# Raw weight tiles in a free activation buffer, and a new written order of the first slots, in a fused attention and MLP kernel

## The chip, the cores and the metric

The kernel runs on one core of a Trainium2 chip. The metric is the device time of one execution in microseconds (us), lower being better. The engines are named as the profile names them: PE is TensorE (matmuls), DVE is VectorE, ACT is ScalarE, POOL is GpSimd, and SP is SyncE, which here only issues DMAs.

## The reference, cut to what matters

```python
# q, k, v: (4, 8, 576, 64) float32; all four MLP weights float64
kv  = np.einsum('bhsd,bhse->bhde', k, v)
out = np.einsum('bhsd,bhde->bhse', q, kv)
rms = np.sqrt(np.mean(out * out, axis=-1, keepdims=True) + 1e-06)
x   = (out / rms * g_norm).astype(np.float32)      # reordered to (2304, 512)

h = x @ w_in                                       # (2304, 2048)
sp = np.where(h > 20.0, h, np.log1p(np.exp(np.minimum(h, 20.0))))
x = (h * np.tanh(sp) @ w_out).astype(np.float32)   # mish, back to (2304, 512)

h = x @ w2_in
g = np.maximum(h, 0.0) + alpha * np.minimum(h, 0.0)
y = (g @ w2_out).astype(np.float32)
```

## The kernel before, in words

**Stages.** An attention without softmax makes the 2304 x 512 activations x, a first MLP (512 to 2048 to 512, with mish) follows, then a second one (with alpha). This case lies in the first 200 us, where attention of the first tokens, the preparation of the first MLP's weights and the first MLP itself run beside each other.

**Tokens and slots.** The first MLP works through blocks of 512, 256, 512, 512 and 512 tokens (BLOCKS, L34), and within a block through 16 slots, one for each 128 of the 2048 hidden features. Slot s holds mm1(s), 12 matmuls into a tile h, and mm2(s - 4), 12 matmuls into four accumulators acc0 to acc3 (L467 to L489). Each product of fp32 numbers is three matmuls, since both operands are split into a high and a low half (`three`, L128 to L132). Between the two, ScalarE makes n = mish(h) (L505) and its high half gh (L498), and VectorE the low half gl (L499).

**Weights.** A weight tile arrives as raw float64, 512 KB: w1(j) by L381, w2(j) by L378. ScalarE scales the high words (`w_scale`, L390), VectorE makes one fp32 word of two in three instructions (`w_bits`, L396, L397, L400, tile wf), ScalarE casts the high half (`w_high`, L435) and VectorE subtracts the low half (`w_low`, L439). A raw tile lies in a ring of three places (`stage`, L363 to L364), and a load has to wait until the last of the three `w_bits` instructions has read what was there. SP issues the loads in their written order, so one that waits holds back those behind it. The raw tiles of the first slots lie elsewhere (`room`, L143).

**x.** The split activations of a block fill one of the two places of the tile x (L353); until block 1 is made the second place is empty.

**What sets the order.** The order of every engine is written out. For the first four slots two tables do it: FIRST (loads; p: k, v and q of a head pair, c: raw chunk of the first four w1 tiles, w4 and w5: w1(4) and w1(5), u0 and u1: w2(0) and w2(1)) and START, with one word for each step: K a kv product, k its copy out of PSUM (L224), l and n the steps of the norm's root (L294 and L297 on ScalarE, L301 on VectorE), x and y the two halves of a quarter of x (L358, L363), Pcj the three matmuls of quarter c of h(j), g mish, G the split of its result, and A, D, H, L scale, bits, high and low half of a weight (Du1 is `w_bits` of w2(1)). Slots 4 to 19 run through `slot` (L961), which plays lists of steps that L884 to L949 fill by slot number; behind that only PE's order is written.

**Banks.** The tile h(3) lies in the PSUM bank of acc3 (L470), so the last three of the 12 matmuls of mm2(0) wait until mish(3) has read h(3).

Of the kernel before, what the change touches and what calls it, by code (L numbers as in the profile page):

```python
# [11 lines left out]
I32 = mybir.dt.int32  # L12
# [13 lines left out]
P = 128  # L26
# [7 lines left out]
EARLY = 4  # L34
WHEN = {1: (8, 3, 1, 2, 3, 6), 2: (4, 4, 1, 2, 3, 6), 3: (0, 5, 1, 2, 4, 5), 4: (0, 5, 1, 2, 4, 5)}
MANUAL = 20
# [3 lines left out]
UNITS = (36, 45, 52, 61, 65, 68, 70, 85)  # L40
ON_POOL = (0, 1, 2, 3, 5)
BY32 = 2
FIRST = "p0 c0 p1 c1 p2 p3 c2 c3 w4 u0 w5 u1".split()
START = """
W9 K0 k0 W1 T0 t0 W2 Ac0 O0 Dc0 s0 W2 K1 M0 k1 Hc0 Lc0 T1 l0 t1 n0 O1 V f0 K2 s1 x0 M1 k2 Ac1 y0 T2 l1
Dc1 t2 n1 O2 f1 K3 s2 Hc1 M2 k3 x1 Lc1 Ac2 T3 y1 l2 P01 Dc2 P02 t3 P12 n2 Hc2 O3 Ac3 f2 s3 M3 Lc2 x2
y2 P00 P03 Dc3 P10 P11 P13 l3 P20 P21 Z n3 Hc3 f3 P22 P23 Lc3 x3 Aw4 y3 Au0 Dw4 P30 P31 P32 P33 g0
G0 Hw4 Lw4 Du0 g1 G1 Hu0 Aw5 Lu0 g2 Dw5 Au1 Hw5 Du1 Lw5
""".split()


# [1 line left out]
def attn_moe_moe2(  # L53
# [30 lines left out]
    nc = tc.nc  # L84
    B, H, S, D = q.shape
    NT, DM = out.shape
# [6 lines left out]
    TM = max(BLOCKS)  # L93
# [11 lines left out]
    xp = ctx.enter_context(tc.tile_pool(name="xp", bufs=2))  # L105
# [17 lines left out]
    acol = const.tile([P, NJ], F32, name="acol")  # L123
# [93 lines left out]
    def kv_of(b, p):  # L217
        return kvs[(NP * b + p) % len(kvs)]

    def kv_ev(b, p):  # L220
        ps = at.pop(("kv", b, p))
        for hs in (slice(0, D), slice(D, P)):
            if b == 0:
                nc.vector.tensor_copy(out=kv_of(b, p)[hs, hs], in_=ps[hs, hs])  # L224
            else:
                nc.scalar.copy(out=kv_of(b, p)[hs, hs], in_=ps[hs, hs])
# [138 lines left out]
    def stage(nm, dt, cols):  # L365
        return st.tile([P, 2 * DM], dt, tag="ws", name=nm, bufs=3)[:, :cols]


    w1, w2 = {}, {}
    wst, wraw = {}, {}  # L370
    home = {}

    def load_w(L, which, j, early=False, s=None):


        s = s if s is not None else room("ws", I32, 2 * DM) if early else stage("ws", I32, 2 * DM)
# [64 lines left out]
    begun = []  # L441
# [162 lines left out]
    def load_unit(i, n):  # L604
        load_w(1, 1, 2 * i + n, s=place(i, f"r{n}"))
# [45 lines left out]
    def load_out(j):  # L651
        load_w(1, 2, j, s=wp.tile([P, 2 * DM], I32, tag=f"w2{j}", name="ws"))
# [232 lines left out]
    for i in range(1, NB):  # L885
# [24 lines left out]
        for p in range(NP):  # L910
            add(hook, h + db + p, b_pe, i, p)
            add(hook, h + db + p, b_ev, i, p)
    early_w = [({"w": 1, "u": 2}[n[0]], int(n[1:])) for n in FIRST if n[0] in "wu"]
    for j in range(NJ):
        if j >= EARLY and (1, j) not in early_w:
            add(late, max(j - 3, EARLY), load_w, 0, 1, j)
            add(mid, j - 2, w_begin, 0, 1, j)
        if (2, j) not in early_w:
            add(early, max(j + 1, EARLY), load_w, 0, 2, j)
            add(last, j + 2, w_begin, 0, 2, j)  # L920
            add(mid, j + 3, w_end)
        add(early, max(NS - NJ + max(j, EARLY) + 1, UNITS[j // 2] + (6 if j // 2 < NU - 1 else 14)), fetch, 1, j)
        t0 = NS - 8 + 3 * j // 2 if j < SOON else NS + OUTS[j - SOON]
        add(early, t0 - (2 if j < SOON else 4), load_out, j)
        add(fin, t0, behind, prep_out, j, j < SOON)
    for i, s in enumerate(UNITS):
        if i in ON_POOL:
            steps, puts = (1, 2, 2, 3, 4, 5), (4, 5, 6)
        else:
            steps, puts = ((1, 2, 2, 2, 3, 4), (3, 4, 5)) if i < NU - 1 else ((3, 4, 7, 7, 8, 11), (8, 9, 12))  # L930
        add(late, s, load_unit, i, 0)
        add(late, s + 1, load_unit, i, 1)
        for step in range(6):
# [11 lines left out]
    for n in range(1, NPASS):  # L945
        t0 = NS + 4 * NU * n
# [93 lines left out]
    with tc.manual_schedule():  # L1040
        nc.scalar.preload_act_table_set("abs_reciprocal_sqrt_and_small")
        for n in FIRST:
            if n[0] == "p":
                load_kv(0, int(n[1]))
                load_q(0, int(n[1]))
            else:
                load_w(0, code[n[0]], int(n[1:]), True)
            if n == "p1":
                for h in range(2):
                    nc.sync.dma_start(out=gcol[h * D : (h + 1) * D, :], in_=g_norm.rearrange("(p o) -> p o", o=1))  # L1050
        nc.sync.dma_start(out=acol, in_=alpha.rearrange("(j p) -> p j", p=P))
        make_identity(nc, ident)
        nc.vector.memset(ones_bd, 0.0)
        nc.vector.memset(ones_m, 0.0)
        for h in range(2):
            r = slice(h * D, (h + 1) * D)
            nc.vector.memset(ones_bd[r, r], 1.0 / D)
            nc.vector.memset(ones_m[r, 16 * h : 16 * h + 16], 1.0 / D)
        nc.vector.memset(epsb, EPS * 2.0**-SHIFT)
        nc.gpsimd.memset(keep[:, : 5 * P], 0.0)  # L1060
        nc.vector.memset(neglo, 0.0)
        for p in range(NP):
            for h in range(2):
                r = 32 * p + 16 * h
                rows = pick[p][:, h * D : (h + 1) * D]
                nc.vector.tensor_copy(out=rows, in_=ident[:, r : r + 1].to_broadcast([P, D]))
                nc.vector.tensor_tensor(
                    out=rows, in0=f32(rows), in1=ident[:, r + 1 : r + 2].to_broadcast([P, D]), op=ALU.add
                )
                nc.vector.tensor_tensor(out=neglo, in0=neglo, in1=ident[:, r + 1 : r + 2], op=ALU.subtract)  # L1070
        for n in START:
            if n[0] in "ADHL":
                w = (0, code[n[1]], int(n[2:]))
                first[n[0]](*w)
            else:
                first[n[0]](*(int(c) for c in n[1:]))
        begun.append((0, 2, 1))
        for s in range(EARLY, MANUAL):
            slot(s)
    with tc.manual_schedule(engines={mybir.EngineType.PE}):  # L1080
# [34 lines left out]
```

## Time and profile before

| | us |
|---|---|
| median of 3 runs | 856.82 (856.34 to 858.07) |
| profiled execution, its own time | 856.71 |
| its span | 854.8 |
| PE busy | 832.7 (97%) |
| DVE busy | 537.1 (63%) |
| ACT busy | 314.1 (37%) |

The span goes from the first to the last instruction on the chip; the execution's own time is 1.9 us longer. A row of the timeline gives an instruction's start, its duration, engine and line, output and input tile, and in brackets how long its engine stood idle before it and what it waited for last. Busy shares over the whole program are means over stages of different kinds, so the stages are looked at apart.

### The profile page before, as it was taken

Reading aid. Unit: us, or ns where it says so; the run is one execution under the profiler, and the core shown is the slowest. Engines: PE = TensorE matmul, PEld = TensorE weight load, DVE = VectorE, ACT = ScalarE, POOL = GpSimd, SP = SyncE. Lnnn points to the kernel's source line nnn. Section 1 sums busy time; section 2 is a strip of 40 time slices with the busy share of each in tenths; the row PEclk is TensorE's granted clock in tenths of the full one; section 3 lists DMA queues with packets and bytes.
Section 4 is the critical chain, followed back from the end, with each engine's and each line's share of the span. In section 5 each row is a group of like instructions: output and inputs, shape, how many; then the busy total and the mean of one; then the engine's idle time right before and its main releaser. Section 6 shows DMA issues by size and latency. Waiting matters only on the chain.

```text
span 854.8 us, 11671 instructions
## 1 busy us (share of the span) xinstructions
PE 832.7 (97%) x4408; PEld 711.5 (83%) x4408; DVE 537.1 (63%) x1017; ACT 314.1 (37%) x619; POOL 41.8 (5%) x52
## 2 busy tenths in 40 slices
PE   7999889989999999999999999999999999999997
PEld 5677668888878887888888888888988988998896
DVE  6988966372246242635697887889665568655644
ACT  4766445434333443234465323234211124111111
POOL 0000000000210303020300000000000000000000
PEclk9999999999999999999999999999999999999999
DMA  9766454414331233026996623241321231411212
GB/s 250 222 172 205 139 150 102 110 27 106 100 112 25 77 109 135 1 94 231 404 357 231 209 63 134 97 137 39 125 61 38 62 123 39 140 44 38 74 38 74
DMA packets 84744, 104.59 MB, mean 122 GB/s; under 512 B 34768, under 2 KB 58832, under 8 KB 84688
## 3 DMA queue, kind: packets, MB, share of 16 engines
q1 hardware_dynamic: 84688, 103.84, 39.2%
q8 instruction: 35, 0.57, 0.3%
q14 instruction: 21, 0.17, 0.1%
HBM read 79.70 MB, written 24.12 MB: 121 GB/s over the span
## 4 chain that ended last, share of the span: by engine, by line
PE 82%; DVE 8%; DMA 4%; SPq 2%; ACT 2%; issue 1%; DVEq 0%; ACTq 0%
PE acc L130 13%; PE acc L132 13%; PE acc L131 13%; PE h L130 7%; PE h L131 6%; PE h L132 6%; PE pp L130 6%; PE pp L132 6%; PE pp L131 6%; DMA v<-in_v_dram 2%; SPq L183 2%; PE kvps L214 1%; DVE wf L397 1%; DVE wf L400 1%; DMA k<-in_k_dram 1%
## 5 line engine op out<-in xcount | busy, mean ns | idle before, releaser
L130 PE MATMUL acc<-gh,w 128*128 128x512 f32 (+1 forms) x320 | 119.6, 374 | 0.8 <-ACT n L505 0.4
L132 PE MATMUL acc<-gh,w 128*128 128x512 f32 (+1 forms) x320 | 118.0, 369 | 0.0
L131 PE MATMUL acc<-gl,w 128*128 128x512 f32 (+1 forms) x320 | 117.9, 369 | 0.0
L499 DVE TENSOR_TENSOR gl<-n,gh 128x512 fp32r<-128x512 f32 (+1 forms) x80 | 52.2, 652 | 89.9 <-ACT gh L498 89.6
L130 PE MATMUL h<-x,w 128*128 128x512 f32 (+1 forms) x240 | 91.5, 381 | 5.6 <-ACT n L505 5.6
L132 PE MATMUL h<-x,w 128*128 128x512 f32 (+1 forms) x240 | 89.7, 374 | 0.6 <-DVE w L439 0.5
L131 PE MATMUL h<-x,w 128*128 128x512 f32 (+1 forms) x240 | 89.6, 373 | 0.0
L132 PE MATMUL acc<-w,g 128*128 128x512 f32 x216 | 85.4, 395 | 0.0
L498 ACT CAST gh<-n 128x512 fp32r<-128x512 f32 (+1 forms) x80 | 46.1, 577 | 100.4 <-PE acc L132 99.9
L766 ACT CAST g<-ty 128x384 fp32r<-128x384 f32 x48 | 24.7, 515 | 138.4 <-DVE ty L764 136.5
L130 PEld LDWEIGHTS acc<-gh,w 128*128 128x128 f32 x320 | 60.3, 188 | 11.9 <-ACT n L505 0.9
L132 PEld LDWEIGHTS acc<-gh,w 128*128 128x128 f32 x320 | 60.3, 188 | 10.6 <-DVE w L439 0.4
L131 PEld LDWEIGHTS acc<-gl,w 128*128 128x128 f32 x320 | 60.4, 189 | 9.6
L505 ACT ACTIVATE n<-h 128x512 f32<-128x512 f32 (+1 forms) x80 | 44.5, 556 | 45.3 <-DVE gl L499 44.6
L130 PEld LDWEIGHTS h<-x,w 128*128 128x128 f32 x240 | 45.9, 191 | 17.3 <-ACT n L505 6.9
L131 PE MATMUL acc<-w,g 128*128 128x512 f32 x144 | 56.6, 393 | 0.0
L131 PE MATMUL acc<-w,xb 128*128 128x512 f32 x144 | 56.6, 393 | 0.0
L130 PE MATMUL acc<-w,g 128*128 128x512 f32 x144 | 56.0, 389 | 0.0
L130 PE MATMUL acc<-w,xb 128*128 128x512 f32 x144 | 56.0, 389 | 0.0
L132 PEld LDWEIGHTS h<-x,w 128*128 128x128 f32 x240 | 45.9, 191 | 9.5 <-DVE w L439 1.6
L131 PEld LDWEIGHTS h<-x,w 128*128 128x128 f32 x240 | 45.8, 191 | 7.4
L132 PEld LDWEIGHTS acc<-w,g 128*128 128x128 f32 x216 | 40.5, 188 | 9.4 <-DVE g L767 0.9
(216 smaller groups left out, 1700.2 us busy)
## 6 DMA issues: line engine op xcount, KB each, us to landing
xb<-wd SPq DMA_DIRECT2D x72, 256.0 KB, 2.7
ws<-in_moe_w_out_dram SPq DMA_DIRECT2D x32, 512.0 KB, 4.3
ws<-in_moe_w_in_dram SPq DMA_DIRECT2D x16, 512.0 KB, 4.8
r<-in_moe_w_in_dram SPq DMA_DIRECT2D x12, 512.0 KB, 3.9
wd<-r SPq DMA_DIRECT2D x12, 512.0 KB, 2.6
w<-wd SPq DMA_DIRECT2D x12, 512.0 KB, 6.0
k<-in_k_dram SPq DMA_DIRECT2D x16, 288.0 KB, 3.8
v<-in_v_dram SPq DMA_DIRECT2D x16, 288.0 KB, 4.2
```

Source lines behind the costliest of these rows:

```text
L130: nc.tensor.matmul(ps, lh, rh, start=start, stop=False, **kw)
L131: nc.tensor.matmul(ps, lh, rl, start=False, stop=False, **kw)
L132: nc.tensor.matmul(ps, ll, rh, start=False, stop=stop, **kw)
L183: nc.sync.dma_start(out=t[r : r + 32, C * p0 : C * (p0 + n)].rearrange("p (b d) -> p b d", d=32), in_=q[b, h, s : s + C * n, d : d + 32].r ...
L214: nc.tensor.matmul(ps[hs, hs], kt[:, h, j, :], vt[:, h, j, :], start=(j == 0), stop=(j == KVJ - 1))
L397: nc.vector.scalar_tensor_tensor(out=si, in0=high, scalar=-0x80000000, in1=si, op0=ALU.bitwise_and, op1=ALU.bitwise_or)
L400: nc.vector.scalar_tensor_tensor(out=si, in0=high, scalar=3, in1=si, op0=ALU.logical_shift_left, op1=ALU.bitwise_or)
L498: nc.scalar.copy(out=gh, in_=g)
L499: nc.vector.tensor_tensor(out=gl, in0=g, in1=f32(gh), op=ALU.subtract)
L505: nc.scalar.activation(out=g, in_=hps.pop(kk)[:, :T], func=AF.Mish)
L766: nc.scalar.copy(out=h, in_=out)
```

## The change

Seven edits.

1. The START order is written anew, and FIRST brings c2 ahead of p3.
2. ON_ACT: the kv copies of head pairs 1, 2 and 3 (two instructions each) go from VectorE to ScalarE.
3. XW: the raw tiles of w1(6) to w1(13) go to four places in the empty x tile (`xw`) instead of the ring of three. w1(6) and w1(7) are loaded at the end of FIRST, w1(8) to w1(13) up to five slots ahead instead of three.
4. w2(j) is loaded one slot earlier, from slot 4 on.
5. w1(14) and w1(15) still go through the ring, loaded three slots ahead as before.
6. Cast and low half of w2(1) (Hu1, Lu1) stand in START instead of slot 4 (`begun.append` is gone).
7. The small load of alpha goes from the start to slot 19.

```diff
-FIRST = "p0 c0 p1 c1 p2 p3 c2 c3 w4 u0 w5 u1".split()
+FIRST = "p0 c0 p1 c1 p2 c2 p3 c3 w4 u0 w5 u1 w6 w7".split()
+ON_ACT = (1, 2, 3)
+XW = range(6, 14)
...
-G0 Hw4 Lw4 Du0 g1 G1 Hu0 Aw5 Lu0 g2 Dw5 Au1 Hw5 Du1 Lw5
...
+Du0 G0 P33 Hw4 Lw4 g1 Hu0 Lu0 G1 g2 Au1 Dw5 Hw5 Lw5 Du1 Hu1 Lu1
...
@@ kv_ev @@
-            if b == 0:
+            if b == 0 and p not in ON_ACT:
                 nc.vector.tensor_copy(out=kv_of(b, p)[hs, hs], in_=ps[hs, hs])
...
+    xw = xp.tile([P, 8 * TM], I32, tag="x", name="xw")
...
@@ load_w @@
+        if s is None and (L, which) == (0, 1) and j in XW:
+            n = (j - XW[0]) % 4
+            s = xw[:, n * 2 * DM : (n + 1) * 2 * DM]
         s = s if s is not None else room("ws", I32, 2 * DM) if early else stage("ws", I32, 2 * DM)
...
-            add(late, max(j - 3, EARLY), load_w, 0, 1, j)
+            add(late, max(j - (5 if j in XW else 3), EARLY), load_w, 0, 1, j)
+        if j > EARLY + 1:
             add(mid, j - 2, w_begin, 0, 1, j)
         if (2, j) not in early_w:
-            add(early, max(j + 1, EARLY), load_w, 0, 2, j)
+            add(early, max(j, EARLY), load_w, 0, 2, j)
...
+    add(early, MANUAL - 1, lambda: nc.sync.dma_start(out=acol, in_=alpha.rearrange("(j p) -> p j", p=P)))
...
-        nc.sync.dma_start(out=acol, in_=alpha.rearrange("(j p) -> p j", p=P))
...
-        begun.append((0, 2, 1))
```

Behind the edits all line numbers are higher by 2 to 8: L390 becomes L397, L396, L397 and L400 become L403, L404 and L407, L435 becomes L442, L439 becomes L446, L505 becomes L512, L381 and L378 become L388 and L385. PE's order changes in START alone: six matmuls of quarter 0 of h go ahead of the third head pair's attention product, and others of START change places. POOL's order stays.

**ScalarE, end of START and slot 4.** Here w20, w21 and w15 are the split tiles of w2(0), w2(1) and w1(5), and n the results of mish. Before, from the cast of w2(0) on:

```order
L435 CAST w20_461<-wf_451 128x512
L390 ACTIVATE ws_140<-ws_140 128x512
L505 ACTIVATE n_465<-h_359 128x512
L390 ACTIVATE ws_142<-ws_142 128x512
L435 CAST w15_472<-wf_467 128x512
L252 COPY qT_513<-tps_510 128x256
L505 ACTIVATE n_519<-h_384 128x512
L390 ACTIVATE ws_515<-ws_515 128x512
L435 CAST w21_526<-wf_474 128x512
```

and now, where n_467 is mish(2) and n_524 mish(3):

```order
L442 CAST w20_460<-wf_444 128x512
L505 CAST gh_463<-n_458 128x512
L512 ACTIVATE n_467<-h_364 128x512
L397 ACTIVATE ws_143<-ws_143 128x512
L442 CAST w15_474<-wf_470 128x512
L442 CAST w21_481<-wf_477 128x512
L254 COPY qT_520<-tps_517 128x256
L512 ACTIVATE n_524<-h_318 128x512
```

The cast of w2(1) has moved from behind mish(3) (n_519 before) to a place ahead of it and ahead of the copy of qT.

**VectorE, the same place.** Here wf_467 (now wf_470) are the bits of w1(5), wf_474 (now wf_477) those of w2(1), wf_522 (now wf_527) those of w1(6). Before:

```order
L396 TENSOR_SCALAR wf_467<-ws_140 128x512
L397 SCALAR_TENSOR_TENSOR wf_467<-ws_140,wf_467 128x512
L400 SCALAR_TENSOR_TENSOR wf_467<-ws_140,wf_467 128x512
L396 TENSOR_SCALAR wf_474<-ws_142 128x512
L397 SCALAR_TENSOR_TENSOR wf_474<-ws_142,wf_474 128x512
L400 SCALAR_TENSOR_TENSOR wf_474<-ws_142,wf_474 128x512
L439 TENSOR_TENSOR w15_472<-wf_467,w15_472 128x512
L396 TENSOR_SCALAR wf_522<-ws_515 128x512
L397 SCALAR_TENSOR_TENSOR wf_522<-ws_515,wf_522 128x512
L400 SCALAR_TENSOR_TENSOR wf_522<-ws_515,wf_522 128x512
L439 TENSOR_TENSOR w21_526<-wf_474,w21_526 128x512
```

and now:

```order
L403 TENSOR_SCALAR wf_470<-ws_141 128x512
L404 SCALAR_TENSOR_TENSOR wf_470<-ws_141,wf_470 128x512
L407 SCALAR_TENSOR_TENSOR wf_470<-ws_141,wf_470 128x512
L446 TENSOR_TENSOR w15_474<-wf_470,w15_474 128x512
L403 TENSOR_SCALAR wf_477<-ws_143 128x512
L404 SCALAR_TENSOR_TENSOR wf_477<-ws_143,wf_477 128x512
L407 SCALAR_TENSOR_TENSOR wf_477<-ws_143,wf_477 128x512
L446 TENSOR_TENSOR w21_481<-wf_477,w21_481 128x512
L403 TENSOR_SCALAR wf_527<-xw_95 128x512
```

The low half of w1(5) has moved ahead of the bits of w2(1), and the low half of w2(1) ahead of the bits of w1(6).

**SP, the last loads of the first MLP's weights.** L381 and L378 (now L388 and L385) are loads of w1 and w2 tiles; ws_955 is w1(13), ws_1012 w1(14), ws_1069 w1(15), and now ws_1006 is w1(14) and ws_1063 w1(15). Before:

```order
L381 DMA ws_955<-in_moe_w_in_dram 128x4x256
L378 DMA ws_994<-in_moe_w_out_dram 128x1024
L381 DMA ws_1012<-in_moe_w_in_dram 128x4x256
L378 DMA ws_1054<-in_moe_w_out_dram 128x1024
L381 DMA ws_1069<-in_moe_w_in_dram 128x4x256
L378 DMA ws_1105<-in_moe_w_out_dram 128x1024
L378 DMA ws_1165<-in_moe_w_out_dram 128x1024
L378 DMA ws_1216<-in_moe_w_out_dram 128x1024
L183 DMA q_1257<-in_q_dram 32x12x32 x4
```

and now, where ws_859, ws_929 and ws_988 are w2(9), w2(10) and w2(11):

```order
L385 DMA ws_859<-in_moe_w_out_dram 128x1024
L385 DMA ws_929<-in_moe_w_out_dram 128x1024
L385 DMA ws_988<-in_moe_w_out_dram 128x1024
L388 DMA ws_1006<-in_moe_w_in_dram 128x4x256
L385 DMA ws_1048<-in_moe_w_out_dram 128x1024
L388 DMA ws_1063<-in_moe_w_in_dram 128x4x256
L385 DMA ws_1099<-in_moe_w_out_dram 128x1024
L385 DMA ws_1159<-in_moe_w_out_dram 128x1024
L385 DMA ws_1210<-in_moe_w_out_dram 128x1024
L185 DMA q_1251<-in_q_dram 32x12x32 x4
```

The load of w1(14) has moved from behind that of w2(10) to behind that of w2(11), and that of w1(15) from behind that of w2(11) to behind that of w2(12). All three places of the ring are held by w2 tiles when the load of w1(14) comes up.

## Rows read from the trace of the kernel before

**Rows 1.** Windows by stage: span, busy us of each engine, granted clock, DMA share.

```profile
24.00:47.00 23.00, 20.87 (x105) 15.03 (x104) 21.24 (x36) 17.02 (x30) 0.00 (x0) 1.00 0.55 163
47.00:84.00 37.00, 37.00 (x235) 29.70 (x235) 31.19 (x53) 24.22 (x53) 0.00 (x0) 1.00 0.74 209
84.00:122.00 38.00, 32.53 (x128) 25.32 (x128) 32.45 (x62) 17.48 (x34) 0.00 (x0) 0.91 0.49 147
122.00:200.00 78.00, 74.00 (x596) 66.73 (x595) 40.85 (x73) 33.59 (x82) 0.00 (x0) 1.00 0.42 91
200.00:855.00 655.00, 649.01 (x3152) 561.41 (x3150) 395.18 (x740) 209.97 (x407) 40.49 (x45) 1.00 0.34 113
```

**Rows 2.** VectorE timeline, start-up: start, us, instruction, idle before, releaser.

```profile
17.11 0.46 DVE L224 COPY keep<-kvps 64x64 f32<-64x64 f32 x2 [0.55 <-PE kvps L214]
...
20.19 0.69 DVE L301 SCALAR_TENSOR_TENSOR u<-mps,u 128x512 f32<-128x512 f32 x1
...
25.97 0.69 DVE L301 SCALAR_TENSOR_TENSOR u<-mps,u 128x512 f32<-128x512 f32 x1
...
34.22 0.70 DVE L363 TENSOR_TENSOR x<-q,x 128x512 fp32r<-128x512 f32 x1
...
37.20 0.69 DVE L499 TENSOR_TENSOR gl<-n,gh 128x512 fp32r<-128x512 f32 x1 [0.42 <-ACT gh L498]
...
43.44 0.42 DVE L396 TENSOR_SCALAR wf<-ws 128x512 int32<-128x512 int32 x1
...
45.29 0.68 DVE L439 TENSOR_TENSOR w<-wf,w 128x512 fp32r<-128x512 f32 x1
```

**Rows 3.** ScalarE timeline, start-up.

```profile
18.89 0.63 ACT L297 ACTIVATE u<-q 128x512 f32<-128x512 f32 x1
...
43.55 0.62 ACT L435 CAST w<-wf 128x512 fp32r<-128x512 f32 x1 [1.00 <-DVE wf L400]
...
44.34 0.60 ACT L505 ACTIVATE n<-h 128x512 f32<-128x512 f32 x1
```

**Rows 4.** TensorE timeline: matmuls that waited.

```profile
44.99 0.50 PE L130 MATMUL acc<-gh,w 128*128 128x512 f32 x1 [0.43 <-ACT n L505]
...
99.47 0.50 PE L130 MATMUL h<-x,w 128*128 128x512 f32 x1 [1.85 <-ACT n L505]
...
116.69 0.64 PE L130 MATMUL h<-x,w 128*128 128x512 f32 x1 [2.76 <-ACT n L505]
...
179.26 0.47 PE L339 MATMUL bps<-yr,picks 128*128 128x512 f32 x1 [1.89 <-DVE yr L333]
```

**Rows 5.** VectorE timeline, slots 8 to 13.

```profile
78.62 0.69 DVE L439 TENSOR_TENSOR w<-wf,w 128x512 fp32r<-128x512 f32 x1 [0.86 <-ACT w L435]
...
99.54 0.69 DVE L400 SCALAR_TENSOR_TENSOR wf<-ws,wf 128x512 int32<-128x512 int32 x1
...
102.05 0.69 DVE L397 SCALAR_TENSOR_TENSOR wf<-ws,wf 128x512 int32<-128x512 int32 x1
...
109.54 0.69 DVE L397 SCALAR_TENSOR_TENSOR wf<-ws,wf 128x512 int32<-128x512 int32 x1
```

**Rows 6.** SyncE timeline: DMA issues.

```profile
81.23 0.37 SPq L381 DMA_DIRECT2D ws<-in_moe_w_in_dram  x1
...
100.30 0.33 SPq L378 DMA_DIRECT2D ws<-in_moe_w_out_dram  x1
...
106.00 0.33 SPq L378 DMA_DIRECT2D ws<-in_moe_w_out_dram  x1
```

**Rows 7.** ScalarE timeline, slots 9 and 13.

```profile
85.08 0.68 ACT L390 ACTIVATE ws<-ws 128x512 f32<-128x512 f32 x1 [0.79 <-DMA ws<-in_moe_w_in_dram]
...
107.27 0.59 ACT L505 ACTIVATE n<-h 128x512 f32<-128x512 f32 x1
```

**Rows 8.** DMA issues, whole program: count, KB each, median us to landing.

```profile
ws<-in_moe_w_in_dram SPq DMA_DIRECT2D x16, 512.0 KB, 4.8
```

**Rows 9.** Windows view, one microsecond at the second fall of the clock.

```profile
117.00:118.00 1.00, 1.00 (x4) 0.70 (x4) 0.82 (x2) 0.66 (x2) 0.00 (x0) 0.50 1.09 267
```

More of the change, by code (lines that the diff above doesn't have):

```diff
@@ L42 @@
 BY32 = 2
-FIRST = "p0 c0 p1 c1 p2 p3 c2 c3 w4 u0 w5 u1".split()
+FIRST = "p0 c0 p1 c1 p2 c2 p3 c3 w4 u0 w5 u1 w6 w7".split()
+ON_ACT = (1, 2, 3)
+XW = range(6, 14)
 START = """
-W9 K0 k0 W1 T0 t0 W2 Ac0 O0 Dc0 s0 W2 K1 M0 k1 Hc0 Lc0 T1 l0 t1 n0 O1 V f0 K2 s1 x0 M1 k2 Ac1 y0 T2 l1
-Dc1 t2 n1 O2 f1 K3 s2 Hc1 M2 k3 x1 Lc1 Ac2 T3 y1 l2 P01 Dc2 P02 t3 P12 n2 Hc2 O3 Ac3 f2 s3 M3 Lc2 x2
-y2 P00 P03 Dc3 P10 P11 P13 l3 P20 P21 Z n3 Hc3 f3 P22 P23 Lc3 x3 Aw4 y3 Au0 Dw4 P30 P31 P32 P33 g0
-G0 Hw4 Lw4 Du0 g1 G1 Hu0 Aw5 Lu0 g2 Dw5 Au1 Hw5 Du1 Lw5
+W9 K0 k0 W1 T0 t0 Ac0 W2 O0 Dc0 s0 W2 K1 M0 Hc0 k1 Lc0 T1 l0 t1 n0 V Ac1 O1 f0 s1 K2 Dc1 x0 M1 k2 T2
+y0 l1 P00 t2 n1 P03 Hc1 O2 f1 Ac2 K3 s2 Dc2 M2 k3 x1 T3 l2 Lc1 P02 y1 t3 P01 n2 Aw4 O3 f2 Ac3 P10 s3
+Dc3 x2 M3 Hc2 P13 l3 Lc2 P11 y2 Z n3 P21 P12 f3 Hc3 P20 P23 Lc3 x3 P22 Au0 y3 Aw5 Dw4 P30 P31 g0 P32
+Du0 G0 P33 Hw4 Lw4 g1 Hu0 Lu0 G1 g2 Au1 Dw5 Hw5 Lw5 Du1 Hu1 Lu1
 """.split()
```

## The prediction, made before the changed kernel was run

> **What bounds the kernel now.** I read the windows by stage first [rows 1]. In each row the reader is to see the span, PE's busy time in it, and the granted clock. From 47 to 84 us PE is busy for 37.00 of 37 us. From 24 to 47 it is busy for 20.87 of 23, and VectorE for 21.24. From 84 to 122 PE has 32.53 of 38 at a mean clock of 0.91, with VectorE at 32.45. From 122 to 200 PE lacks 4.00 us, and in the 655 us from 200 on only 5.99. Work behind slot 19 is the same as before, so the change can move time in the first 200 us alone: in the start-up and between 84 and 122, where VectorE sets the pace, and not at 47 to 84, where PE does.
>
> The timelines come second. In the start-up VectorE runs almost without a gap: in the rows from 17.11 to 45.29 [rows 2] brackets stand only at 17.11 (0.55 us) and 37.20 (0.42). The end of the start-up is PE's wait for mish(3): the matmul into the accumulator that shares h(3)'s bank starts at 44.99 after 0.43 us idle [rows 4]. Its mish is at 44.34 on ScalarE, behind the cast of w1(5) at 43.55 [rows 3]. At 78.62 VectorE waits 0.86 us for a ScalarE cast [rows 5]; that cast stands behind kv copies that wait for PE, so VectorE's position is tied to PE's there and a shift of PE goes on into the next stage. Between 84 and 122 PE waits 1.85 and 2.76 us for mish results [rows 4]. VectorE is the late one there: between 78.62 and 109.54 it goes from one weight to the next.
>
> **Term 1, the start-up: +1.6 us.** Removed from VectorE: three pairs of kv copies, of which one costs 0.46 us at 17.11 with 0.55 idle before it [rows 2]. Without it the norm step L301 of pair 1 comes earlier, though not before its input u from ScalarE, ready at 18.89 + 0.63 = 19.52 [rows 3]: a gain of 20.19 - 19.52 = 0.67. The next round, 25.97 - 20.19 = 5.78 us, holds another copy of about 0.46: 5.3 are left. By the low half of the last quarter of x (34.22) VectorE is then 0.67 + 0.46 = 1.1 us ahead, at 33.1. The copies on ScalarE cost nothing on the path, as ScalarE is busy for 17.02 of 23 us [rows 1].
>
> From there to the bits of w2(1) the new order adds work. The wait of 0.42 at 37.20 goes, since the bits of w2(0) now come first. But the low half of w1(5), 0.68 us at 45.29, now stands ahead of the bits of w2(1) and waits for its cast, 0.62 [rows 2, 3]: 0.68 + 0.62 - 0.42 = +0.88. Before, those bits ended where that low half starts, at 45.29; now at 45.29 - 1.1 + 0.88 = 45.07.
>
> Then ScalarE. Before, mish(3) followed the cast of w1(5), whose bits ended at 43.44 where the next row starts; cast, copy of qT and mish took from 43.55 to 44.34 + 0.60 = 44.94, so 1.39 us. In the new order the cast of w2(1) stands in that place, and it can't start before 45.07 + 0.11. mish(3) ends at 45.07 + 0.11 + 1.39 = 46.57 in place of 44.94: +1.6 us. mish(3) was ready to run long before (h(3) needs no late weight); only the queue holds it. PE, which stood idle for 0.43 us there, now stands about 2.0, or up to 3 if it arrives earlier. From 47 to 84 nothing can win this back, because PE has no gap.
>
> The bounds: if the copies give nothing (PE runs six matmuls ahead of the third attention product, and pair 3's data lands behind c2's 512 KB), the term is +2.7; if they give 2.0 (all three pairs with their idle time), it is +0.7. I take 1.1, nearest to the two rows of L301.
>
> **Term 2, w1(14): +2.9 us.** Up to w1(13) the raw tiles leave the ring, so their loads wait for less. But w1(14) still goes through it, and all three places are then held by w2 tiles. The order shows its load behind that of w2(11). Its place is that of w2(9), free when L400 at 99.54 has run (0.69). In the trace of before a load waited for exactly this event and was issued at 100.30 [rows 6]. A load of w1 issued at 81.23 was awaited by its scale step at 85.08 [rows 6, 7]: 3.85 us to landing. So landing is at 104.15, the scale takes 0.68 and ends at 104.83, and the second instruction of the bits, which needs it, starts at about 104.95. Before, it started at 102.05 [rows 5], directly behind other VectorE work. The difference is 2.9 us, on top of the 1.6 that everything here has moved by. Behind the waiting instruction stand VectorE's low halves, the bits of w2(10) and the x of the next block, and mish at 107.27 [rows 7] and its matmuls wait for them. VectorE stays the late engine until PE's wait at 116.69, so PE gets the 2.9 in full.
>
> **Term 3, w1(15): +1.1 us.** It needs the place of w2(10). The load that waited for this before was issued at 106.00 [rows 6]; with the 2.9 of term 2 at 108.9. Landing 3.85 later at 112.75, scale 0.68, bits' second instruction at 113.5. Without a wait it would be at 109.54 + 2.9 = 112.4 [rows 5]. That leaves +1.1. With the whole program's median of 4.8 us to landing [rows 8] the terms are 3.85 and 2.05. From below, 2.0 for both together if VectorE had slack that I don't see, and zero if another load's release served them.
>
> The Trainium skill bears on this in the page "DMA: Bandwidth & Descriptors", section "Anatomy of one DMA": a transfer costs about 2.0 us fixed plus its bytes over 436 GB/s, which makes an estimate of 3.2 us for 512 KB (its fit is of transfers that GpSimd issues, here SP issues them). The trace's 3.85 is longer and decides; by the page's figure terms 2 and 3 would be 2.25 and 0.45 and the time about 861.1 us.
>
> **What costs nothing.** The earlier loads of w1(6) to w1(13) and of w2 end DMA waits of ScalarE such as the 0.79 us at 85.08 [rows 7], but VectorE, for which it works, has no gap beside it. The load of alpha is small and used far later. Loads of w1(6) and w1(7) in the start add 1 MB at a DMA share of 0.55 [rows 1]. q of block 2 is loaded later, since SP now waits for w2(15)'s place, but two weights' work stands before its use.
>
> **Sum.** 1.6 + 2.9 + 1.1 = 5.6 us. The profiled execution took 856.71 us, which makes 862.3; the median of the runs is 0.1 higher, which makes 862.4.
>
> **Rivals.**
> - The clock falls in the new pause. At 117 us the granted clock is 0.50, the lower level of 1.2 GHz, after PE's wait of 2.76 us [rows 9, 4]; over the stage from 84 the mean of 0.91 over 38 us makes 3.4 us lost [rows 1], two falls of 1.7, and the waits of 1.85 and 2.76 are the two. But after 1.89 us idle at 179.26 [rows 4] the stage's mean clock is 1.00. A pause of 2 to 3 us at 46 lies between. A fall costs 1.7, as PE is the bound from there: 862.4 + 1.7 = 864.1. The Trainium skill, "TensorE: Matmul & The Clock Gate", Part 1, says that the throttled state is the default and activity releases it; the trace agrees as far as the fall at 117 goes.
> - Only the start costs. The two loads get their places early enough, or VectorE has slack: 856.8 + 1.6 = 858.4. Against it stands the order, in which the loads wait for named releases.
> - The start gains its 1.1 us (mish(3) isn't late, because ScalarE or h(3) was what counted), and terms 2 and 3 stand: 856.8 - 1.1 + 4.0 = 859.7.
> - Faster. The early loads let VectorE enter 84 with a lead, so PE's 1.85 us at 99.47 goes, the start gains 1.1, and the last two raw tiles are hidden: 856.8 - 2.95 = 853.9. It decides if VectorE at 78.62 no longer waits for ScalarE, thus if its lead comes from loads. The row at 78.62 says that ScalarE's cast was late, not a load, and no row of VectorE there names a DMA [rows 5]. In the same page on DMA the skill's section "Rules for kernel authors" says to issue a DMA early and wait for it late, which this change does for eight tiles; for the two left in the ring it does the reverse.
>
> **How the numbers follow.** Forecast 0.51, own range 860.8 to 863.7; clock 0.18; only the start 0.12; faster 0.10; start gains 0.09. From 857.8 to 865.0 the range leaves out the faster case (0.10), about 0.04 of the 858.4 case, and about 0.06 above. 0.2%, about what a measurement of this kernel can tell from no change, is 1.7 us: 855.1 to 858.5. The case at 858.4 lies half inside, which with a few hundredths of the others makes 0.08 for the same, 0.09 faster and 0.83 slower.
>
> **What would show it.** Right, step by step: PE's first matmul into the accumulator of h(3) starts near 46.6 after an idle time of 2 us or more, released by mish; ScalarE's cast before that mish waits for VectorE's bits. The scale of w1(14) near 105.8 waits for a DMA, and VectorE's bits behind it; the same for w1(15) near 114.4. PE's longest waits are then in slots 13 to 16, and from 200 us on both traces run alike. Wrong: the load of w1(14) issued well before 101, VectorE without a DMA wait between 100 and 116, or PE's accumulator matmul before 45. If the first quarter of x on VectorE isn't earlier than before, term 1 is larger; if the granted clock falls between 46 and 52, the clock's case holds.

## The result and the profile after

The changed kernel takes 867.99 us in the median of 4 runs (866.39 to 869.24), the kernel before 857.32 on the same chip: a ratio of 1.0124, with an interval of 1.0102 to 1.0146. It is slower by 10.7 us. The forecast was 862.4 with a range up to 865.0. The direction was right, and the size too small by half.

The profiled execution took 868.76 us, with a span of 867.0, thus 12.2 more than the 854.8 of before. The windows of the kernel after, with stage borders moved along with the work, answer to [rows 1] (columns as there):

```profile
24.00:47.00 23.00, 18.75 (x85) 13.15 (x82) 20.49 (x34) 16.26 (x28) 0.00 (x0) 1.00 0.80 249
47.00:86.00 39.00, 39.00 (x253) 31.46 (x251) 29.78 (x51) 24.36 (x54) 0.00 (x0) 0.96 0.61 174
86.00:124.00 38.00, 29.98 (x125) 23.00 (x124) 29.94 (x57) 15.69 (x30) 0.00 (x0) 0.91 0.30 95
124.00:212.00 88.00, 80.92 (x608) 72.99 (x607) 44.87 (x80) 35.80 (x85) 0.00 (x0) 0.94 0.43 90
212.00:867.00 655.00, 649.23 (x3154) 561.59 (x3152) 395.21 (x740) 210.24 (x407) 40.43 (x45) 1.00 0.34 113
```

From 212 on PE is as busy as before in the 655 us behind 200. What is new stands ahead of it: PE's share falls at 24 to 47 and 86 to 124, and the granted clock is below 1.00 in two stages where it was 1.00, at 47 to 86 (0.96) and 124 to 212 (0.94).

PE's timeline in the kernel after shows the waits; the first four and the last answer to [rows 4]:

```profile
46.55 0.50 PE L132 MATMUL acc<-gh,w 128*128 128x512 f32 x1 [2.73 <-ACT n L512]
...
102.51 0.50 PE L132 MATMUL h<-x,w 128*128 128x512 f32 x1 [1.85 <-ACT n L512]
...
113.62 0.80 PE L132 MATMUL h<-x,w 128*128 128x512 f32 x1 [4.09 <-ACT n L512]
...
123.42 0.50 PE L132 MATMUL h<-x,w 128*128 128x512 f32 x1 [1.40 <-ACT n L512]
...
141.78 0.50 PE L134 MATMUL acc<-gh,w 128*128 128x512 f32 x1 [2.38 <-DVE w L446]
...
165.70 0.39 PE L132 MATMUL h<-x,w 128*128 128x256 f32 x1 [1.38 <-ACT n L512]
...
190.36 0.64 PE L341 MATMUL bps<-yr,picks 128*128 128x512 f32 x1 [1.89 <-DVE yr L335]
```

These matmuls are milestones: the same instruction can be found in every trace, and the stretch between two of them is a price that an offset of the start doesn't touch. 102.51, 113.62 and 123.42 begin mm1(13), mm1(14) and mm1(15), as 99.47, 107.92 and 116.69 do in the kernel before; 190.36 (179.26 before) is the first matmul bps of block 2, called bps below. The row of the kernel before that [rows 4] don't have:

```profile
107.92 0.51 PE L130 MATMUL h<-x,w 128*128 128x512 f32 x1 [0.37 <-ACT n L505]
```

| stretch on PE (us) | before | after | difference | predicted |
|---|---|---|---|---|
| start to acc of h(3) | 44.99 | 46.55 | +1.56 | +1.6 |
| from there to mm1(13) | 54.48 | 55.96 | +1.48 | 0 |
| mm1(13) to mm1(14) | 8.45 | 11.11 | +2.66 | +2.9 |
| mm1(14) to mm1(15) | 8.77 | 9.80 | +1.03 | +1.1 |
| mm1(15) to bps | 62.57 | 66.94 | +4.37 | 0 |
| from there to the end | 675.54 | 676.64 | +1.10 | 0 |
| span | 854.8 | 867.0 | +12.20 | +5.6 |

The three predicted terms came within 0.3 us each. 6.95 us lie in stretches that the prediction gave nothing. The first row alone holds an offset of the start, which differs between executions. ScalarE's timeline at the first place, answering to [rows 3]:

```profile
45.11 0.62 ACT L442 CAST w<-wf 128x512 fp32r<-128x512 f32 x1 [2.55 <-DVE wf L407]
45.63 0.37 ACT L254 COPY qT<-tps 128x256 f32<-128x256 f32 x1
45.90 0.60 ACT L512 ACTIVATE n<-h 128x512 f32<-128x512 f32 x1
```

The cast of w2(1) waits 2.55 us for VectorE, and mish(3), whose input has long been there, is queued two places behind it. VectorE's timeline (answering to [rows 5]) shows the ring's waits and a later one:

```profile
107.07 0.43 DVE L403 TENSOR_SCALAR wf<-ws 128x512 int32<-128x512 int32 x1 [2.43 <-DMA ws<-in_moe_w_in_dram]
107.76 0.69 DVE L404 SCALAR_TENSOR_TENSOR wf<-ws,wf 128x512 int32<-128x512 int32 x1 [0.26 <-ACT ws L397]
...
115.47 0.43 DVE L403 TENSOR_SCALAR wf<-ws 128x512 int32<-128x512 int32 x1 [0.67 <-DMA ws<-in_moe_w_in_dram]
...
140.43 0.71 DVE L248 STREAM_TRANSPOSE qT<-q 128x512 f32<-128x512 f32 x1 [3.87 <-DMA q<-in_q_dram]
141.07 0.65 DVE L446 TENSOR_TENSOR w<-wf,w 128x512 fp32r<-128x512 f32 x1
```

The last two lines belong together: the transpose of q waits for its DMA, and the low half of a weight, for which PE waits until 141.78, is the next instruction in VectorE's order. SyncE's timeline says why q is late (answering to [rows 6]; a row's duration runs over all its instructions):

```profile
103.33 0.38 SPq L388 DMA_DIRECT2D ws<-in_moe_w_in_dram  x1
...
111.71 0.38 SPq L388 DMA_DIRECT2D ws<-in_moe_w_in_dram  x1
117.75 11.00 SPq L385 DMA_DIRECT2D ws<-in_moe_w_out_dram  x3
128.80 3.90 SPq L185 DMA_DIRECT2D q<-in_q_dram  x8
...
133.71 5.08 SPq L185 DMA_DIRECT2D q<-in_q_dram  x8
```

The first two are w1(14) and w1(15). Then SP issues w2(13), waits with w2(14) and w2(15) for places in the ring until 128.4, and only then the loads of q of block 2, eight for the first head pair and eight for the second. In the kernel before w2(15) stood behind them, and SyncE's timeline has

```profile
115.15 3.90 SPq L183 DMA_DIRECT2D q<-in_q_dram  x8
...
120.06 4.08 SPq L183 DMA_DIRECT2D q<-in_q_dram  x8
```

The transpose that waits is the second pair's: loads of q in this stretch land at most 4.8 us behind their issue (4.0 before), so the first pair's had long landed by 140.43. This transpose belongs to slot 20, from where on only PE's order is written. Its place among VectorE's instructions is therefore not fixed by the listing and differs between the runs below.

### The profile page after: what moved, and what is told of

The parts are those of the page before. It is cut to its first block, busy times and chain, and to the rows that moved or that the text cites. A ratio compares the mean times of both kernels' runs of the same rounds, so it can differ in the third digit from the quotient of the medians.

```text
span 867.0 us, 11663 instructions
## 1 busy us (share of the span) xinstructions
PE 838.7 (97%) x4408; PEld 716.9 (83%) x4408; DVE 535.8 (62%) x1011; ACT 315.1 (36%) x625; POOL 41.7 (5%) x52
## 4 chain that ended last, share of the span: by engine, by line
PE 81%; DVE 9%; DMA 3%; SPq 2%; ACT 2%; issue 1%; DVEq 0%; ACTq 0%
PE acc L134 13%; PE acc L132 13%; PE acc L133 13%; PE h L132 7%; PE h L134 6%; PE h L133 6%; PE pp L132 6%; PE pp L134 6%; PE pp L133 6%; SPq L185 2%; PE kvps L216 1%; DVE wf L404 1%; DVE wf L407 1%; DMA q<-in_q_dram 1%; DMA v<-in_v_dram 1%
## 5 line engine op out<-in xcount | busy, mean ns | idle before, releaser
L505 ACT CAST gh<-n 128x512 fp32r<-128x512 f32 (+1 forms) x80 | 46.2, 578 | 106.7 <-PE acc L134 106.2
L132 PEld LDWEIGHTS h<-x,w 128*128 128x128 f32 x240 | 46.6, 194 | 20.2 <-ACT n L512 9.9
L512 ACT ACTIVATE n<-h 128x512 f32<-128x512 f32 (+1 forms) x80 | 44.5, 556 | 44.6 <-DVE gl L506 44.1
L134 PEld LDWEIGHTS h<-x,w 128*128 128x128 f32 x240 | 46.8, 195 | 10.9 <-DVE w L446 3.1
L133 PEld LDWEIGHTS h<-x,w 128*128 128x128 f32 x240 | 46.7, 195 | 7.5
```

What stands on the lines that cost most here:

```text
L132: nc.tensor.matmul(ps, lh, rh, start=start, stop=False, **kw)
L133: nc.tensor.matmul(ps, lh, rl, start=False, stop=False, **kw)
L134: nc.tensor.matmul(ps, ll, rh, start=False, stop=stop, **kw)
L505: nc.scalar.copy(out=gh, in_=g)
L512: nc.scalar.activation(out=g, in_=hps.pop(kk)[:, :T], func=AF.Mish)
```

## The experiments

Ratios are to the kernel before on the same chip.

**1. Cast of w2(1) behind mish(3) again**

```diff
-... Du1 Hu1 Lu1
+... Du1
+        begun.append((0, 2, 1))
```

> The changed kernel, with the cast and low half of w2(1) (Hu1, Lu1) taken out of START and put back into slot 4, behind mish(3). My theory: PE's wait of 2.73 us at 46.55 was mish(3) standing behind that cast, and the fall of the clock from 47 to 50.6 came from that wait. Both go: about 2.7 + 1.5 = 4.2 us less than the changed kernel's 868.0, so 863.8, with the matmul into the accumulator of h(3) at about 43.9 and a granted clock of 1.00 from 47 to 51. Rival: VectorE alone sets the pace up to 124 us, and PE's pause cost nothing: 868.0.

862.55 us, 1.0056 (1.0039 to 1.0073), so 0.68% less than the changed kernel, 5.8 us by the medians' ratios; 4.2 were expected. In PE's timeline no wait is left between the low half of w1(4) and mm1(13):

```profile
38.94 0.50 PE L134 MATMUL h<-x,w 128*128 128x512 f32 x1 [1.53 <-DVE w L446]
...
98.00 0.50 PE L132 MATMUL h<-x,w 128*128 128x512 f32 x1 [1.85 <-ACT n L512]
```

mm1(13) starts 102.51 - 98.00 = 4.5 us earlier, and the clock is 1.00 from 42 to 96; 0.5 us of this is an offset, as the second kv product began at 10.67 and not at 11.20. In the traces the rest lies behind mm1(15): from there to bps it is 183.74 - 118.89 = 64.85 us in place of 66.94, and behind bps 0.88 less. The clock falls of 166 and 190 us in the changed kernel have no counterpart here. The edit doesn't touch those places, so this part looks like chance; no run shows it apart. The theory holds: a pause of PE at 46 goes through to the end.

**2. The pause filled with matmuls**

```diff
+            if kk == 0 and m == 3:
+                hps[5] = bank("h", "h")
+                for _ in range(11):
+                    nc.tensor.matmul(hps[5][:, :T], w1[0, 0][0][:, :P], xh[0, 0], start=True, stop=True)
```

> The changed kernel with eleven further matmuls, whose results nothing uses, ahead of the matmul that waits for mish(3): PE works through 2.5 of the 2.73 us of its pause and the pause's end stays where it is. This takes the clock apart from the wait. If the pause made the clock fall and the half-clock stretch cost time: granted clock 1.00 from 47 to 51, and 1.5 us less than 868.0, so 866.5. If the clock falls for another reason, or what it cost is hidden behind VectorE: 868.0.

866.1 us, 1.0101 (1.007 to 1.0133). The medians fell by 2 us, but the interval overlaps the changed kernel's, so by time alone it is unclear. The stretch in the trace is not. PE no longer stands idle ahead of acc of h(3) (this execution was 1.3 us later from the start):

```profile
47.90 0.50 PE L132 MATMUL acc<-gh,w 128*128 128x512 f32 x1 [0.22 <-ACT n L516]
```

mm1(13) follows at 102.40, 54.50 us later as in the kernel before, and the clock of the windows from 42 to 96 us is 1.00. In the traces of 3 and 4, which keep the pause (2.73 and 2.74 us), the clock falls behind it too and the stretch is 56.00 us in both. So of the 3.04 us that the start cost, 1.48 were the clock's. In the kernel after, the windows behind the pause read (columns as above):

```profile
47.00:48.00 1.00, 1.00 (x9) 0.43 (x9) 0.87 (x2) 0.26 (x2) 0.00 (x0) 0.57 0.00 0
48.00:49.00 1.00, 1.00 (x24) 1.00 (x20) 1.00 (x2) 0.42 (x1) 0.00 (x0) 0.50 0.00 0
49.00:50.00 1.00, 1.00 (x6) 0.79 (x4) 0.49 (x2) 0.72 (x3) 0.00 (x0) 0.50 0.02 8
```

PE is busy throughout, at the lower of its two levels, after 2.73 us of idleness.

**3. w2(15) behind q**

```diff
-            add(early, max(j, EARLY), load_w, 0, 2, j)
+            add(early, max(j + (j == NJ - 1), EARLY), load_w, 0, 2, j)
```

> The changed kernel with the load of w2(15) alone put back by one slot, behind the loads of q and kv of block 2. My theory after the result: SP held these loads at 117.75 to 128.75 behind the wait of w2(15)'s load for its place in the ring, VectorE's transpose of q at 140.43 waited 3.87 us for them and PE 2.38 us at 141.78, and later 1.38 at 165.70, with two falls of the clock. These go: about 4.4 us less than 868.0, so 863.6, q issued near 118. Rival: w2(15) then becomes late in its turn, or q was late only because the whole stage is late: 868.0.

865.61 us, 1.0092 (1.0064 to 1.0119): 0.32% less, where 0.5% was expected; the interval overlaps the changed kernel's (1.0102 to 1.0146) a little, so the time alone leaves it open. q is issued at 122.60 and not near 118, as the whole stage is late by the ring. The stretch from mm1(15) to bps is 187.30 - 124.13 = 63.17 us in place of 66.94, 3.8 of the 4.4 us. The times give back less, 2.7 us, and the 3.8 holds chance: the same late q stands in the traces of 1, 2 and 8, where the stretch is 64.85, 67.88 and 64.42 us. It is long where the clock fell a second time, at 166 (changed kernel and 2), and shorter where it did not (1 and 8). A late q thus cost 1.9 to 5.3 us over the kernel before. With the load, the transpose's place on VectorE changed as well: it stands behind a low half again, as in the kernel before.

**4. w1(14) in the x tile**

```diff
-XW = range(6, 14)
+XW = range(6, 15)
-            add(late, max(j - (5 if j in XW else 3), EARLY), load_w, 0, 1, j)
+            add(late, max(j - (5 if j in XW else 4), EARLY), load_w, 0, 1, j)
```

> The changed kernel with the raw tile of w1(14) in the x tile too, and w1(15) loaded four slots ahead instead of three, so that it gets the place that w1(14) had. My theory: VectorE's waits for a DMA at 107.07 (2.43 us) and 115.47 (0.67) were the ring's, with the scale steps behind them 3.7 us on the path. They go, PE's wait at 113.62 shrinks from 4.09 to about 0.4, and the stage ends 3.7 us earlier: 864.3. Rival: the raw tiles only expose what VectorE's other work would have cost, and less than 1 us goes: 867 or more.

862.97 us, 1.0053 (1.0032 to 1.0073): 0.71%, or 6.1 us less, with 3.7 expected. PE between mm1(13) and mm1(15):

```profile
103.61 0.50 PE L132 MATMUL h<-x,w 128*128 128x512 f32 x1 [1.88 <-ACT n L512]
...
120.88 0.50 PE L132 MATMUL h<-x,w 128*128 128x512 f32 x1 [2.73 <-ACT n L512]
```

17.27 us, as against 20.91 after and 17.22 before: 3.64 for the ring. The surplus is the next stretch, 182.27 - 120.88 = 61.39 us against 66.94. SyncE and VectorE:

```profile
126.26 3.94 SPq L185 DMA_DIRECT2D q<-in_q_dram  x8
```

```profile
134.73 0.69 DVE L446 TENSOR_TENSOR w<-wf,w 128x512 fp32r<-128x512 f32 x1 [0.69 <-ACT w L442]
...
137.71 0.71 DVE L248 STREAM_TRANSPOSE qT<-q 128x512 f32<-128x512 f32 x1 [1.00 <-DMA q<-in_q_dram]
```

q is not earlier here: its loads begin 5.38 us behind mm1(15), as in the changed kernel (128.80 - 123.42). What differs is VectorE's order. The low half for which PE waited 2.38 us now stands ahead of the transpose, PE doesn't wait for it, and the clock is 1.00 from 110 to 230 us. So in the changed kernel the late q cost time through what stood behind its transpose on VectorE. This place is no edit of its own in any run; that it alone would do is not shown.

**5. All three edits**

> The changed kernel with the three edits of the first experiments at once: cast of w2(1) back behind mish(3), w2(15) loaded behind q of block 2, w1(14) in the x tile and w1(15) a slot earlier. Theory: the loss is the sum of three places (start with its clock fall, ring, q), read in the traces of the single edits as 4.5, 3.6 and 3.8 us, and nothing else is lost. Then 868.0 - 11.9 = 856.1, about 2 us below the kernel before, whose runs on this chip had a median of 858.0; that surplus is VectorE's saved copies in the start. As freeing the ring alone also brought q earlier, ring and q may overlap, and the two together give no more than 7.4. Rival: what is won ahead of 84 us is lost again where VectorE sets the pace, and the sum of the edits is no better than the best one, 862.5.

856.84 us, 0.9999 (0.9987 to 1.001). The three edits undo the whole loss: the sum of 1, 3 and 4 would have been 1.71%, and 1.25% came, since 3 and 4 act on the same stretch behind mm1(15), and a part of what 1 gave back lies there too. The 2 us expected below the kernel before did not appear. PE's waits at mm1(13) and mm1(15), 1.86 and 2.74 us, are those of [rows 4].

**6. mish(3) early, and the low half of w1(4) earlier**

It has the edits of 3 and 4, and besides them this order (mish(3) is now the g3 in START and no longer runs in slot 4):

```diff
-... g0 P32 Du0 G0 P33 Hw4 Lw4 g1 Hu0 Lu0 G1 g2 Au1 Dw5 Hw5 Lw5 Du1 Hu1 Lu1
+... g0 P32 P33 G0 Hw4 Lw4 Du0 g1 Hu0 Lu0 G1 g2 Au1 g3 Dw5 Hw5 Lw5 Du1 Hu1 Lu1
```

> The changed kernel with w1(14) in the x tile, w1(15) a slot earlier and w2(15) behind q, and the end of START ordered anew: mish(3) stands ahead of the casts of w1(5) and w2(1), and the low half of w1(4) ahead of the bits of w2(0). Theory: PE's wait of 1.5 us for the low half of w1(4) at 38.9 goes too, and as PE is the bound from 47 to 84, most of it stays: 1 to 1.5 us below the run with the three edits, so about 855. Rival: VectorE's order only moves the wait to the first matmul of w1(5) or of w2(1), and the time is that of the three edits, 856.1.

858.28 us, 1.0013 (1.0 to 1.0026): no gain, the theory was wrong and the rival came nearer. The wait for the low half of w1(4) is gone, but VectorE now waits three times for a cast that it has to follow at once (here of VectorE):

```profile
40.00 0.69 DVE L446 TENSOR_TENSOR w<-wf,w 128x512 fp32r<-128x512 f32 x1 [0.69 <-ACT w L442]
...
43.77 0.69 DVE L446 TENSOR_TENSOR w<-wf,w 128x512 fp32r<-128x512 f32 x1 [0.69 <-ACT w L442]
...
46.94 0.69 DVE L446 TENSOR_TENSOR w<-wf,w 128x512 fp32r<-128x512 f32 x1 [0.69 <-ACT w L442]
```

PE reaches mm1(13) at 98.64 and 100.52 in the runs 6 and 5 (run 5 began its second kv product 0.84 us later), but bps at 179.09 and 179.74: the 1 us won ahead of 84 was given back behind it. Why the timed runs are 0.14% above those of 5 stays open.

**7. The kernel before with the copies on ScalarE alone**

```diff
-            if b == 0:
+            if b == 0 and p not in (1, 2, 3):
```

> The kernel before with one part of the change: the kv copies of head pairs 1, 2 and 3 go to ScalarE, START as it was. Theory: VectorE gains about 1.1 us by the low half of the last quarter of x, as the changed kernel's trace showed 0.85 to 1.1, and PE's waits in the start shrink by 0.4 to 1.1: 0.8 us less than the kernel before, 0.999 of it, close to what can be told from no change. Rival: ScalarE's copies delay its norm steps, and nothing is won: 1.000.

858.75 us, 1.002 (1.001 to 1.0029): slower by 0.2%, opposite to what I expected. In its trace, counted from the second kv product (11.84, and 10.97 before), the last low half of x on VectorE is at 23.52 us, and was at 23.25 before: VectorE lost its copies and waited for ScalarE's casts instead, up to 2.43 us at 13.95. A further part, 2.45 us of PE at 130.45, came from a q that was late in this execution. In the changed kernel that low half, at 33.37, is 1.1 us earlier than before when counted likewise (33.37 - 11.20 = 22.17, against 23.25), and 0.85 us as the rows stand. So the copies by themselves don't bring this; what the new order brings without them was not run.

**8. The kernel before with the loads alone**

It has XW, w6 and w7 in FIRST and w2(j) a slot earlier, as in the diff of the change, and nothing else.

> The kernel before with the loads of the change alone: raw tiles of w1(6) to w1(13) in the x tile, loaded as in the changed kernel, w2(j) a slot earlier; START's table, copies and the cast of w2(1) as before. Theory: it shows the waits for w1(14) and w1(15) (about 3.7 us) and the late q of block 2 (about 3.8) without the start's loss: 7.5 us more than the kernel before, a ratio of 1.0087, PE's wait ahead of mm1(14) about 4 us. Rival: with VectorE's start as it was the releases come at other times and the loads cost 2 us or less, or even gain by the prefetch: 1.002 or less.

863.8 us, 1.0078 (1.006 to 1.0096); 1.0087 was expected. PE:

```profile
46.42 0.50 PE L131 MATMUL acc<-gh,w 128*128 128x512 f32 x1 [0.45 <-ACT n L510]
...
112.24 0.79 PE L131 MATMUL h<-x,w 128*128 128x512 f32 x1 [4.34 <-ACT n L510]
...
140.22 0.50 PE L133 MATMUL acc<-gh,w 128*128 128x512 f32 x1 [2.24 <-DVE w L444]
```

The start waits 0.45 us as before, mm1(14) waits 4.34, and the weight behind q 2.24. The loads lose time without the new START; the new START's loss without the loads was not run.

**9. Low halves on GpSimd, with the three edits**

```diff
-        nc.vector.tensor_tensor(out=l, in0=s, in1=f32(h), op=ALU.subtract)
+        e = nc.gpsimd if (L, which) == (0, 2) and 6 <= j <= 12 else nc.vector
+        e.tensor_tensor(out=l, in0=s, in1=f32(h), op=ALU.subtract)
```

> The run with the three edits, and besides the low halves of w2(6) to w2(12), seven subtractions, go from VectorE to GpSimd, which is idle there. Theory: with ring and q mended VectorE alone sets the pace from 84 to 122, and its 7 x 0.6 = 4.2 us less let PE's waits of 1.86, 0.68, 1.50 and 2.74 us shrink by about that: 4 us below the run with the three edits, a ratio of 0.995 to the kernel before. Rival: the two engines slow each other or the low halves come too late from GpSimd, and the time stays at 0.999 to 1.001.

858.51 us, 1.0009 (0.9992 to 1.0027): nothing gained, so the rival holds. GpSimd's timeline:

```profile
77.23 1.29 POOL L447 TENSOR_TENSOR w<-wf,w 128x512 fp32r<-128x512 f32 x1 [75.36 <-ACT w L442]
...
100.11 1.48 POOL L447 TENSOR_TENSOR w<-wf,w 128x512 fp32r<-128x512 f32 x1 [8.01 <-ACT w L442]
```

and VectorE's at the same times:

```profile
77.74 1.33 DVE L404 SCALAR_TENSOR_TENSOR wf<-xw,wf 128x512 int32<-128x512 int32 x1 [0.96 <-ACT xw L397]
...
100.66 1.48 DVE L404 SCALAR_TENSOR_TENSOR wf<-xw,wf 128x512 int32<-128x512 int32 x1 [0.21 <-ACT xw L397]
```

The VectorE instruction that falls into GpSimd's takes 1.33 and 1.48 us in place of 0.69, and so loses about what the move saved. VectorE is busy for 37.72 us from 78 to 122, against 37.67 in the run with the three edits.

**10. The kernel before with w2(15) ahead of q**

```diff
-            add(early, max(j + 1, EARLY), load_w, 0, 2, j)
+            add(early, max(j + (j < NJ - 1), EARLY), load_w, 0, 2, j)
```

> The kernel before with one thing of the change: the load of w2(15) goes a slot earlier, ahead of q and kv of block 2. It prices the step that the prediction took for free. Theory: SP waits with that load for the bits of w2(12), which end at 121.6 in the kernel before, q is issued near 122 instead of 115.15, VectorE's transposes wait some 3 us for it and PE 2 us, and a fall of the clock may come on top: 2 to 4 us more than the kernel before, 1.002 to 1.005, the stretch from mm1(15) to the first bps matmul near 64.6 us instead of 62.57. Rival: q's lateness matters only where ring and start have already made the stage late: 1.000.

858.31 us, 1.001 (0.9997 to 1.0023): 0 to 2 us, less than I expected. q goes out at 122.00 and VectorE's first transpose waits until 134.20, with the low half behind it as in the changed kernel, but PE's wait is only this:

```profile
135.54 0.50 PE L132 MATMUL acc<-gh,w 128*128 128x512 f32 x1 [1.29 <-DVE w L439]
```

The clock doesn't fall behind it, and from mm1(15) (116.63) to bps (179.07) it is 62.44 us, as before. q is not earlier here: its transpose starts 17.57 us behind mm1(15), and 17.01 in the changed kernel. But the stretch begins at the lower clock level, as in the kernel before, so PE comes later and q's lateness is partly covered; in the changed kernel it begins at the higher one, PE waits 2.38 us, and two falls follow.

**11. The kernel before with those low halves on GpSimd**

> The kernel before with nothing of the change and the low halves of w2(6) to w2(12) on GpSimd. Theory: VectorE was the bound from 84 to 122 before as well, so 3 to 4 us less than the kernel before, 0.996. Rival: its raw tiles in the ring of three then arrive too late, and it gains less than 1 us while the run with the raw tiles in the x tile gains 4.

857.79 us, 1.0008 (0.9995 to 1.0022): nothing, for the same reason as in 9: VectorE's instructions beside GpSimd's take 1.21 to 1.48 us. It gains less than 1 us as the rival said, but not by the ring, as 9 gained nothing either.

**12. The kernel before with the mended loads**

> The kernel before with the change's loads, mended: raw tiles of w1(6) to w1(14) in the x tile, w1(15) four slots ahead, w2(15) behind q of block 2; START, copies and the cast of w2(1) as before. It tells what the prefetch is worth by itself. Theory: VectorE had no gap for a raw tile before, so an earlier tile buys nothing: 1.000 (0.999 to 1.001), PE's stretch from mm1(12) to mm1(15) at 17.2 us as before. Rival: the prefetch gives something of its own, which the new START of the run with the three edits then lost again: 0.997 or less.

857.64 us, 0.9997 (0.9983 to 1.0011). The prefetch by itself is worth nothing that can be told here. The stretch named in the expectation (it begins with mm1(13)) is 118.55 - 101.27 = 17.28 us.

## Why the prediction was right in direction and too small in size

**Start, +1.6.** Right: +1.56, acc of h(3) at 46.55 where 46.57 was worked out. The head of the queue did it, as experiment 1 shows. That the two agree to 0.02 us is luck. Two parts were off by 0.25 us and cancelled: x was 0.85 and not 1.1 us earlier as the rows stand, and the work from there to the bits of w2(1) grew by 0.63 (33.37 to 45.07, before 34.22 to 45.29) and not by 0.88. And the start differs between executions: this matmul stands at 46.55, 47.28 and 47.61 in the traces that keep the new START and its pause (changed kernel, 3, 4), and at 44.99, 44.92 and 44.67 in those that keep the old start with its loads (kernel before, 10, 11), so the term lies between 1.6 and 2.9 us. That the copies on ScalarE cost nothing on the path was wrong by itself: in experiment 7 VectorE waits up to 2.43 us for ScalarE instead.

**w1(14) and w1(15), +2.9 and +1.1.** Right: 2.66 and 1.03, and no luck, as the five traces with this ring (changed kernel, 1, 2, 3, 8) give 2.66 to 2.89 and 0.89 to 1.03. The load of w1(14) was issued at 103.33 and its scale began at 107.06:

```profile
107.06 0.67 ACT L397 ACTIVATE ws<-ws 128x512 f32<-128x512 f32 x1 [3.14 <-DMA ws<-in_moe_w_in_dram]
```

These are 3.73 us to landing, where the row of before gave 3.85. The estimate of 3.2 us by the Trainium skill ("DMA: Bandwidth & Descriptors", "Anatomy of one DMA") is shorter than both, and they decide. Experiments 4 and 8 show the ring as the cause.

**"What costs nothing": q of block 2.** This step failed. It put the later q at nothing, since two weights' work stands before its use. In the kernel before q was issued from 115.15 on, the second pair's from 120.06, and VectorE's row reads

```profile
126.03 0.71 DVE L246 STREAM_TRANSPOSE qT<-q 128x512 f32<-128x512 f32 x1 [3.04 <-DMA q<-in_q_dram]
```

so VectorE waited for q already, hidden from PE but with no slack left. I had not read that stage's waits. In the changed kernel q was issued 13.65 us later, 6.92 more than mm1(15), its transpose waited 3.87 us with a low half behind it, PE waited 2.38 us for that, and the stretch cost 4.37 us; experiment 3 gives 3.8 of it back. Experiments 4 and 10 show the limit of this: with the low half ahead of the transpose the stretch costs nothing, and on the old schedule the same order of loads costs 0 to 2 us.

**The clock, taken as a rival at 0.18.** It came true. The sum of the forecast left it out. Behind the pause at 46 it fell, for 1.48 us (1.7 were estimated), and experiments 1 and 2 show the pause to be the cause. It fell again after the waits of 2.38 and 1.38 us; behind 190.36, where the kernel before kept 1.00 after the same 1.89 us, the windows of the kernel after show it again:

```profile
190.00:192.00 2.00, 1.64 (x7) 1.57 (x8) 0.96 (x2) 0.17 (x1) 0.00 (x0) 0.62 0.00 0
192.00:194.00 2.00, 2.00 (x11) 1.90 (x10) 0.69 (x1) 0.44 (x1) 0.00 (x0) 0.52 0.00 0
```

That is most of the last +1.10, and no fixed price of that wait: the 1.89 us stand ahead of bps in all 14 traces, and a fall follows in four of them (changed kernel, 3, 6, 9). Summed over the windows of 1 us from 36 to 230, the clock takes 3.4 us in the kernel before and 10.2 in the kernel after; where PE would have waited anyway, this cost nothing. Whether a given pause is followed by a fall differs from run to run: the mean clock of the changed kernel's four executions was 0.988 to 0.992, with the longer times at 0.988. What share of the median's 10.7 us is the clock's can't be said exactly. From the one trace it is 1.48 in the first stretch, and some part of the 4.37 and 1.10.

**The other rivals.** "Only the start", "start gains" and "faster" all fell with the ring's two waits and mish(3). The range ended at 865.0 since the clock's case was priced as one fall and q at nothing.

## What to carry to other kernels

When a load is moved ahead in an in-order issue queue, read the waits of everything that it now precedes: a transfer whose consumer already waits in the trace of before has no slack, however much work seems to stand ahead of it. Then read what stands behind that consumer on its engine, and who waits for that. If a prefetch takes some tiles out of a ring, look at the ones that stay, since they meet places filled by another stream. A pause of 2 to 3 us on TensorE is to be priced with a fall of the clock that may follow it (about 1.5 us here), above all where TensorE is the bound afterwards.

## What the runs showed of the hardware that was not expected

- GpSimd held VectorE up in experiments 9 and 11. Beside a GpSimd subtraction of 128x512 (1.27 to 1.49 us) a VectorE instruction that takes 0.69 us alone took 1.31 to 1.48, and one that takes 0.42 alone took 1.23 and 1.41. The Trainium skill, "SBUF — State Buffer", section "SBUF: two separate sides", says that of a GpSimd operation that reads SBUF and a VectorE operation with two SBUF inputs the one that starts first holds the shared ports and the other fully blocks; the trace agrees, VectorE's instruction, which has two such inputs and starts second, ending 0.55 us behind GpSimd's (77.74 + 1.33 = 79.07, and 77.23 + 1.29 = 78.52).
- q of block 2's second head pair, eight transfers, was used 6.0 us after its first issue in the kernel before (120.06 to 126.03) and 6.7 us after (133.71 to 140.43), where a weight tile of 512 KB took 3.7; SP needed 4.1 and 5.1 us for the eight issues alone.
- The same wait of PE, 1.89 us ahead of bps, was followed by the lower clock level in four traces and not in the ten others. A wait of 2.73 to 2.76 us ahead of mm1(15) was followed by it in the kernel before, 5 and 10, and not in 4, 6 and 7, where it was 2.73, 2.73 and 2.74.
